# Attention then a squared-ReLU layer on one core: exp sums of batch 0's first query half as TensorE products by ones, and a new written order of the front

## The chip, the core and the metric

The kernel runs on one core of one Trainium2 chip. TensorE (PE in the profile) multiplies matrices out of the on-chip buffer into PSUM, VectorE (DVE) and ScalarE (ACT) do elementwise work, GpSimd (POOL) and SyncE (SP) issue most of the DMAs here. Each engine takes its own instructions from its own queue in the written order, and engines wait for one another by semaphores. The metric is device time in microseconds (us); lower is better. Times in the trace are counted from the start of the profiled span.

## The reference

```python
# q, k, v: (8 batches, 12 heads, 448 tokens, 64)
scores = scale * q @ k.T                 # per batch and head
e = exp(scores - max)
attn = e / (sum(e) + exp(-max) + 1e-9)   # softmax with a one added
x = (attn @ v) as (8 * 448, 768)
out = square(relu(x @ w_in)) @ w_out     # w_in 768 x 2048, w_out 2048 x 768
```

The kernel leaves out the maximum: it computes `exp(scores)`, and divides by the sum plus one.

## The kernel before, in words

A head is 64 wide, so most attention products are 64x64 tiles, four of which fit on TensorE's 128x128 array: two halves of rows, two halves of columns. The kernel groups four heads to a "quad" (`g`, three to a batch): a quad has two pairs `j` of heads and two heads `i` to a pair. The 448 keys are seven chunks `c` of 64.

Batch 0 is worked in two halves of 224 queries, so that work can begin early. A half of a quad (`half`, `g`) has four visits `k`, and visit number n = 12·half + 4·g + k (`HALVES`, L259). So n = 0 to 11 are the first half of quads 0, 1, 2, and n = 12 to 23 the second half. From n = 24 on come the quads of batch 1, with seven visits each. Visits with k = 3 hold one chunk instead of two; in the first half of quad 0 (`pieces`, L262) visits 0 and 1 take pair j = 0 and visits 2 and 3 take pair j = 1, so that each lies in one half of the columns when it is multiplied by the values.

The order of the first part is written out by hand as a string, `ORDER` (L858); a loop (L875) calls one function for each word. A word is a letter and numbers; each issues instructions on one engine, and the engine runs them in that order. The words that matter here:

| word | function | engine | what |
|---|---|---|---|
| `c`, `t`, `u` | `first_cast`, `first_transpose`, `first_copy` | ACT/DVE, PE, DVE/ACT | quad 0's queries and keys cast, transposed, copied |
| `Tb,g,n` | `transpose_one` (L204) | PE | 14 transposes of queries (n=0) or keys (n=1) of quad g, batch b |
| `Ub,g,n,c0,c1,act` | `transposed_copy` (L211) | DVE, or ACT with act=1 | chunks c0 to c1 of them, PSUM to the buffer |
| `sn` | `half_scores` (L272), `quad_scores` | PE | scores of a visit, 8 products at most, 4 for a visit with k = 3 |
| `en` | `half_exp` (L298), `quad_exp` | ACT | exp of a visit, 128x896 or 128x448 |
| `pn` | `post` (L313) | PE | exps times values of a visit; 28 products for a half of a quad |
| `bm,step` | `half_add` (L335) | DVE | four adds that bring the seven chunks of exps to one (m = 3·half + g) |
| `ym` | `half_sum` (L350) | PE | that one by ones: 4 products |
| `zm`, `nm` | `half_z` (L362), `half_reciprocal` (L371) | ACT | Ln(sum + one), exp of the negative |
| `xm` | `half_x` (L375) | DVE | values' products times the reciprocal |
| `ihalf,pair` | `half_in` (L529) | PE | 12 products of `x` with `w_in` for one half of batch 0's queries |
| `j`, `k`, `l`, `r`, `g` | `later_in` and its ReLU and square | PE, ACT or DVE, DVE | the first layer's products and what follows them |
| `dn` | a load | POOL | one or two DMAs |
| `S0` | `sums_of_quad` (L449) | PE | first sums of batch 1 |

Three PSUM pools bind the front. `s_psum` (L62) has two buffers: scores n can only be written when the exp of the visit that held the buffer has run. `x_psum` (L64) has one buffer, a pair of banks, for values and sums of a half of a quad: the next half of a quad waits for `x` of the one before. `m_psum` (L65) has two banks, for transposes and other products; the first half of quad 1 keeps its values and sums there.

From `S0` on nothing in the order of the words differs between the two kernels. The `d` words, the loads, stand in the same order in both.

Of the kernel before, what the change touches and what calls it, by code (L numbers as in the profile page):

```python
# [17 lines left out]
def kernel(  # L18
# [183 lines left out]
    tps = {}  # L202
# [651 lines left out]
    def other_ring():  # L854
# [240 lines left out]
```

## Time and profile before

| | |
|---|---|
| median of 3 runs | 372.84 us (372.32 to 373.31) |
| the profiled execution's own time | 372.36 us |
| its span in the profile | 370.3 us |
| PE busy | 361.7 us, 98% of the span |
| ACT busy | 282.4 us, 76% |
| DVE busy | 275.7 us, 74% |
| granted TensorE clock | 1.0 throughout |

The span is shorter than the time by 2.06 us, which lie around it. Busy PE time counts a matmul from its start to its modelled end, so overlapping products and gaps smaller than a pipeline's depth are not seen in it; the start times of the rows tell more. A row of the timeline gives the start, the time from the first start to the last end of a run of like instructions, engine, line, operation, shape and count, and in brackets the engine's idle time before it with what ended that.

### The profile page before, as it was taken

To read this page: it belongs to the slowest core of one execution; us is meant where nothing else is said; L and a number is where in the kernel's file an instruction comes from. 1 tells how busy PE (TensorE), PEld (TensorE's weight loads), DVE (VectorE), ACT (ScalarE), POOL (GpSimd) and SP (SyncE) were. 2 spreads that over 40 slices of the span, in tenths; PEclk is the share of its full clock that TensorE was granted. 3 is DMA by queue.
4 is the path that set the end of the run, shared out by engine and by line. 5 is a ranking of instruction groups with operands and counts; after the bars stand their busy time and mean duration, and the time that the engine had idled before them with its cause. 6 is when DMAs were issued, how large, how long until landed. Compare 5 with 4: busy or idle time off the path is not lost.

```text
span 370.3 us, 13666 instructions
## 1 busy us (share of the span) xinstructions
PE 361.7 (98%) x6024; PEld 248.8 (67%) x6024; DVE 275.7 (74%) x484; ACT 282.4 (76%) x413; POOL 62.3 (17%) x96
## 2 busy tenths in 40 slices
PE   8789999999999999999999999999999999999996
PEld 4566556669977755567799965557777765555664
DVE  3888898999987875867887874777878777885441
ACT  6899988987899645689999665679999748794221
POOL 8543350400400330400201060400200000000000
PEclk9999999999999999999999999999999999999999
DMA  8999999999777999905229669854212110001232
GB/s 138 203 205 205 204 198 206 226 225 189 154 146 133 190 181 191 134 2 114 62 58 156 154 118 180 162 64 99 61 53 66 47 62 5 2 0 44 86 85 88
DMA packets 75052, 45.31 MB, mean 122 GB/s; under 512 B 47473, under 2 KB 72945, under 8 KB 74993
## 3 DMA queue, kind: packets, MB, share of 16 engines
q0 software_dynamic: 24752, 22.62, 38.7%
q1 hardware_dynamic: 49952, 21.59, 27.0%
q8 instruction: 47, 0.77, 0.9%
q10 hardware_dynamic: 288, 0.23, 0.2%
q14 instruction: 13, 0.10, 0.1%
HBM read 45.69 MB, written 17.93 MB: 172 GB/s over the span
## 4 chain that ended last, share of the span: by engine, by line
PE 90%; ACT 4%; DVE 2%; DMA 2%; issue 1%; POOL 1%; POOLq 0%; DVEq 0%
PE mp L94 42%; PE mp L663 38%; PE sp L94 9%; ACT et L255 3%; DMA nn<-in_k_dram 2%; PE mp L208 1%; ACT rcp L373 1%; DVE qk L218 0%; ACT rcp L366 0%; DVE half L342 0%; DVE half L441 0%; DVE half L443 0%; DVE half L445 0%; DVE half L348 0%; DVE xt L485 0%
## 5 line engine op out<-in xcount | busy, mean ns | idle before, releaser
L255 ACT ACTIVATE et<-sp 128x896 f16<-128x896 f32 (+2 forms) x173 | 145.2, 899 | 7.6 <-PE sp L94 6.9
L94 PE MATMUL mp<-wout,gs 64*64 64x384 f16 (+1 forms) x2736 | 138.8, 322 | 0.2 <-issue 0.2
L94 PEld LDWEIGHTS <-gs 64*64 64x64 f16 (+1 forms) x2736 | 87.4, 107 | 21.7 <-issue 0.8
L663 PEld LDWEIGHTS <-win 128*128 128x128 f16 x480 | 46.4, 98 | 33.6 <-issue 1.2
L94 PE MATMUL sp<-qk 64*64 64x224 f16 (+1 forms) x1056 | 56.2, 273 | 2.3 <-issue 0.7
L663 PE MATMUL mp<-xt,win 128*128 128x448 f16 (+1 forms) x288 | 54.2, 329 | 0.0
L94 PEld LDWEIGHTS <-qk 64*64 64x64 f16 x1056 | 34.4, 114 | 14.5 <-issue 6.2
L189 POOL COPY flatq<-qk 64x384 f16<-64x384 f16 x20 | 15.3, 763 | 159.4 <-DMA qk<-stage_k 142.7
L94 PE MATMUL mp<-et,vn 64*64 64x448 f16 (+1 forms) x616 | 38.8, 345 | 0.0
L663 PE MATMUL mp<-et,win 128*128 128x448 f16 x144 | 32.8, 352 | 0.0
L576 DVE TENSOR_SCALAR ot<-mp 128x384 f32<-128x384 f32 x34 | 18.9, 556 | 18.0 <-PE mp L94 17.9
L663 PE MATMUL mp<-et,nn 128*128 128x448 f16 (+1 forms) x160 | 32.3, 350 | 0.0
L663 PEld LDWEIGHTS <-nn 128*128 128x128 f16 x216 | 21.0, 98 | 14.7
L666 ACT ACTIVATE qk<-mp 128x448 f32<-128x448 f32 (+1 forms) x33 | 16.8, 532 | 16.0 <-PE mp L663 15.9
L580 DVE SCALAR_TENSOR_TENSOR ot<-mp,ot 128x384 f32<-128x384 f32 x42 | 23.4, 556 | 6.7 <-ACT ot L574 4.0
L485 DVE TENSOR_TENSOR xt<-mp,rcp 128x448 f16<-128x448 f32 x42 | 24.2, 618 | 4.3 <-ACT rcp L464 2.2
L94 PEld LDWEIGHTS <-vn 64*64 64x64 f16 x756 | 22.7, 107 | 6.1 <-issue 0.5
L715 ACT ACTIVATE gs<-mp 128x448 f16<-128x448 f32 x28 | 14.2, 543 | 15.0 <-PE mp L663 13.3
L439 DVE TENSOR_TENSOR half<-et 128x1792 f16<-128x1792 f16 x21 | 23.0, 1097 | 1.2 <-ACT et L255 1.2
L660 DVE CUSTOM_DVE_ANT_0 gs<-mp,rcp 128x448 f16<-128x448 f32 x24 | 14.2, 619 | 13.0 <-ACT rcp L666 7.4
L441 DVE TENSOR_TENSOR half<-half,et 128x1792 f16<-128x1792 f16 x21 | 22.8, 1085 | 0.7 <-DVE half L439 0.5
L710 ACT ACTIVATE gs<-gs 128x448 f16<-128x448 f16 (+1 forms) x36 | 22.4, 657 | 1.1 <-DVE gs L660 1.1
(102 smaller groups left out, 450.2 us busy)
## 6 DMA issues: line engine op xcount, KB each, us to landing
out_dram<-ot SPq DMA_DIRECT2D x52, 96.0 KB, 3.5
out_dram<-ot SPq DMA_DIRECT2D x19, 192.0 KB, 2.0
win<-in_moe_w_in_dram POOLq DMA_DIRECT2D x8, 384.0 KB, 12.9
wout<-in_moe_w_out_dram POOLq DMA_DIRECT2D x4, 768.0 KB, 11.8
vn<-in_v_dram POOLq DMA_DIRECT2D x10, 288.0 KB, 5.6
stage_q<-in_q_dram POOLq DMA_DIRECT2D x4, 676.0 KB, 11.6
stage_k<-in_k_dram POOLq DMA_DIRECT2D x4, 676.0 KB, 14.4
nn<-in_q_dram POOLq DMA_DIRECT2D x8, 224.0 KB, 7.9
```

What stands on the lines that cost most here:

```text
L94: return nc.tensor.matmul(out_, lhsT, rhs, start=start, stop=stop)
L189: nc.gpsimd.tensor_copy(km[rows_].rearrange("p h (x o) -> p h x o", o=2)[:, :, :, odd], src[:, :, S // 2 - 32:S // 2])
L255: nc.scalar.activation(out=out_, in_=in_, func=AF.Exp, scale=scale)
L439: nc.vector.tensor_add(esq[m], a[:, 0:w], a[:, w:2 * w])
L441: nc.vector.tensor_add(esq[m], esq[m], z[:, 0:w])
L485: nc.vector.tensor_mul(xts[b][:, 2 * g + i, :], xqs[m][i][:, 0:S], zqs[m][:, i, :])
L576: nc.vector.tensor_scalar(out=ot, in0=op[:, 0:w], scalar1=OUT_SCALE, scalar2=None, op0=ALU.mult)
L580: nc.vector.scalar_tensor_tensor(out=ot, in0=lo[:, 0:w], scalar=OUT_SCALE, in1=ot, op0=ALU.mult, op1=ALU.add)
L660: nc.vector._custom_dve(TENSOR_ADD_SAT, out=out_, in0=ps, in1=t, s0=3.0e38, s1=0.0)
L663: nc.tensor.matmul(out_, lhsT=lhsT, rhs=rhs, start=begins and first, stop=last, skip_group_check=not begins)
L666: nc.scalar.activation(out=t[:, 0:w], in_=src[:, 0:w], func=AF.Copy, scale=scale_)
L710: nc.scalar.activation(out=out_, in_=out_, func=AF.Square)
```

## The change

The sums of the exps of the first query half (n = 0 to 11) are no longer made by adds on DVE (`b0`, `b1`, `b2`) and one set of four products (`y0`, `y1`, `y2`). `post` now also multiplies each piece of exps by ones, right behind its products by the values, into the sums' half of the same PSUM bank. For the second half of the queries nothing changes. `transposed_copy` may now copy the chunks in any order. The words before `S0` are ordered anew; two ReLUs swap engines (`k16` from ACT to DVE, `k17` from DVE to ACT).

```diff
     def transposed_copy(b, g, which, c0=0, c1=KC, act=0):
-        tp = tps.pop((b, g, which)) if c1 == KC else tps[b, g, which]
+        tp = tps[b, g, which]
+        copied[b, g, which] = copied.get((b, g, which), 0) + c1 - c0
+        if copied[b, g, which] == KC:
+            del tps[b, g, which]
...
                 mm(xz[i][64 * j:64 * j + 64, 0:FIRST], vns[0][r, j, g, c, :], e[r, j, c], start=key not in opened, stop=False)
                 opened.add(key)
-
-    SUMS_ON_PE = ()
-    ess = {}
+        if half == 0:
+            for c, j in parts:
+                done[g, j] = done.get((g, j), 0) + 1
+                for i in range(2):
+                    r = slice(64 * i, 64 * i + 64)
+                    mm(xz[i][64 * j:64 * j + 64, FIRST:2 * FIRST], ones[r], e[r, j, c], start=False, stop=done[g, j] == KC)
+
+    done, ess = {}, {}
...
     def half_sum(g, half):
-        xz, e = xzs[g, half], half_e(g, half)
-        t = ess.pop((g, half))[:, 0:4 * FIRST].rearrange("p (j c n) -> p j c n", j=2, c=2)
-        parts = [t[:, :, 0], t[:, :, 1], e[:, :, 6]] if half in SUMS_ON_PE else [t[:, :, 0]]
-        for n, part in enumerate(parts):
-            for i in range(2):
-                for j in range(2):
-                    r = slice(64 * i, 64 * i + 64)
-                    mm(xz[i][64 * j:64 * j + 64, FIRST:2 * FIRST], ones[r], part[r, j], start=False, stop=(n == len(parts) - 1))
+        xz = xzs[g, half]
+        t = ess.pop((g, half))[:, 0:4 * FIRST].rearrange("p (j c n) -> p j c n", j=2, c=2)[:, :, 0]
+        for i in range(2):
+            for j in range(2):
+                r = slice(64 * i, 64 * i + 64)
+                mm(xz[i][64 * j:64 * j + 64, FIRST:2 * FIRST], ones[r], t[r, j], start=False, stop=True)
...
     ORDER = """
-        d0 W8 d8 d1 c1,4,0 c0,0,1 t0,0,0 c1,0,1 t1,0,0 u0,0,0,0 t1,0,4 u1,0,0,0 c0,4,1 u1,0,4,1 t0,0,4 d2 s0 t0,1,0 u0,0,4,1 u0,1,0,0 t1,1,0
-        u1,1,0,0 d10 d9 s1 t0,1,4 e0 t1,1,4 e1 s2 e2 u0,1,4,0 s12 e12 u1,1,4,0 T0,1,0 T0,1,1 U0,1,0,0,4,0 U0,1,1,0,4,0 U0,1,1,4,7,0
-        U0,1,0,4,7,0 s3 s4 p2 p0 e3 b0,0 e4 s6 p1 d18 p3 s5 e6 e5 b0,1 b0,2 T0,2,0 b0,3 y0 T0,2,1 U0,2,0,0,4,0 z0 n0 U0,2,1,0,4,0 b1,0 s8
-        U0,2,0,4,7,0 U0,2,1,4,7,0 x0 d3 d17 d16 b1,1 s9 d15 T1,0,1 e8 e9 U1,0,1,0,7,0 T1,0,0 U1,0,0,0,7,0 b2,0 s11 e11 s10 s13 e10 e13 s14 p8
-        b2,1 p4 d5 b2,2 p9 s7 e14 p10 b2,3 p11 y2 p5 e7 z2 b1,2 p6 s15 b1,3 p7 e15 y1 b3,0 n2 x2 b3,1 z1 s17 e17 b3,2 p12 p13 b3,3 n1 s18 p14
-        s16 e18 p15 x1 y3 T1,1,0 U1,1,0,0,7,0 e16 b4,0 z3 b4,1 s19 e19 i0,6 n3 r0,6,0 s20 e20 s21 i0,7 s22 x3 b4,2 e21 p16 b4,3 e22 b5,0
-        r0,7,0 p17 p18 p19 d4 b5,1 g0,6 y4 z4 n4 s23 T1,1,1 e23 d13 s27 b5,2 x4 i0,4 s28 p20 p21 g0,7 b5,3 e27 p22 p23 y5 U1,1,1,0,7,0 e28 z5
-        r0,4,0 n5 x5 s26 s29 e26 j20,0,2 j23,0,2 j23,2,4 j20,2,4 j20,4,6 e29 j23,4,6 s25 k23,1 s24 g0,4 e25 e24 k20,0 P0 i1,7 j19,0,2 l23 a0,0
-        s32 e32 a0,1 s36 d6 j19,2,4 e36 j16,0,2 l20 j19,4,6 j17,0,2 s34 s33 k19,1 r1,7,0 j17,2,4 j16,2,4 a0,2 l19 e34 j17,4,6 e33 j16,4,6 g1,7
-        s30 d11 k16,1 s31 e30 k17,0 T2,0,0 T1,2,0 T2,0,1 T1,2,1 l16 s35 e31 U2,0,0,0,7,0 U1,2,0,0,7,0 s37 U2,0,1,0,7,1 e35 j18,0,2 j18,2,4 e37
-        j18,4,6 a0,3 i1,6 d19 S0 U1,2,1,0,7,0 v0,0 a1,0 v0,1 Z0 v0,2 l17 v0,3 v0,4 v0,5 k18,0 d7 d12 v0,6 s40 s43 M0 r1,6,0 j27,0,2 a1,1 e43
+        c1,4,0 c0,0,1 W8 d0 c1,0,1 c0,4,1 t0,0,0 t1,0,0 u0,0,0,0 d8 u1,0,0,0 t1,0,4 t0,0,4 u1,0,4,1 u0,0,4,1 d1 s0 d2 t0,1,0 t1,1,0 u0,1,0,0 s1
+        u1,1,0,0 e0 e1 t0,1,4 s2 t1,1,4 u0,1,4,0 d10 s12 T0,1,0 e2 u1,1,4,0 e12 U0,1,0,4,7,0 s13 T0,1,1 s14 e13 d9 U0,1,1,0,4,0 s3 e14
+        U0,1,1,4,7,0 U0,1,0,0,4,0 s4 d18 T0,2,0 e3 s5 U0,2,0,0,4,0 e4 e5 T0,2,1 s6 U0,2,1,0,4,0 s8 d3 e6 U0,2,1,4,7,0 e8 d17 p2 p3 d16 s10
+        U0,2,0,4,7,0 p0 p1 s17 b3,0 e10 T1,0,1 s19 T1,0,0 e17 s7 U1,0,1,0,7,0 z0 U1,0,0,0,7,0 e19 e7 p4 s11 n0 s9 p5 p6 p7 e11 e9 x0 d15 b3,1 z1
+        p8 s15 p9 s21 p10 e15 p11 d5 n1 s20 z2 e20 b3,2 x1 s22 n2 e21 T1,1,0 x2 T1,1,1 s16 p12 e22 e16 p13 d4 p14 p15 b3,3 s18 y3 U1,1,1,0,7,0
+        i0,7 e18 z3 s27 s24 U1,1,0,0,7,0 b4,0 n3 b4,1 i0,6 d13 b4,2 d6 e27 x3 e24 p16 s23 b4,3 e23 p17 p18 p19 r0,7,0 y4 b5,0 z4 b5,1 s26 n4 d11
+        i0,4 b5,2 e26 s32 e32 x4 p20 p21 p22 p23 b5,3 y5 s28 s33 z5 g0,7 r0,6,0 d19 n5 r0,4,0 e28 g0,6 e33 j20,0,2 j23,0,2 g0,4 j23,2,4 j20,2,4
+        x5 j23,4,6 j20,4,6 k20,0 k23,1 s30 s25 P0 i1,7 j17,0,2 e30 s29 e25 s31 l23 r1,7,0 j16,0,2 j19,0,2 a0,0 e29 j19,2,4 j17,2,4 j19,4,6
+        j17,4,6 j16,2,4 j16,4,6 s36 e31 a0,1 a0,2 s34 T1,2,1 k16,0 T1,2,0 k19,1 l19 g1,7 k17,1 T2,0,1 T2,0,0 e36 l16 U1,2,0,0,7,0 e34 l20
+        U2,0,0,0,7,0 s37 s35 j18,0,2 U2,0,1,0,7,1 a0,3 j18,2,4 e37 j18,4,6 i1,6 e35 S0 U1,2,1,0,7,0 v0,0 a1,0 v0,1 Z0 v0,2 l17 v0,3 v0,4 v0,5
```

More of the change, by code (lines that the diff above doesn't have):

```diff
@@ L200, in quad_columns @@
         return qk_of(b)[rows_, n, 2 * S * g:2 * S * (g + 1)].rearrange("p (i c x) -> p c i x", i=2, c=KC)
-    tps = {}
+    tps, copied = {}, {}
     def transpose_one(b, g, which):
@@ L867 @@
-        s32 e32 a0,1 s36 d6 j19,2,4 e36 j16,0,2 l20 j19,4,6 j17,0,2 s34 s33 k19,1 r1,7,0 j17,2,4 j16,2,4 a0,2 l19 e34 j17,4,6 e33 j16,4,6 g1,7
-        s30 d11 k16,1 s31 e30 k17,0 T2,0,0 T1,2,0 T2,0,1 T1,2,1 l16 s35 e31 U2,0,0,0,7,0 U1,2,0,0,7,0 s37 U2,0,1,0,7,1 e35 j18,0,2 j18,2,4 e37
-        j18,4,6 a0,3 i1,6 d19 S0 U1,2,1,0,7,0 v0,0 a1,0 v0,1 Z0 v0,2 l17 v0,3 v0,4 v0,5 k18,0 d7 d12 v0,6 s40 s43 M0 r1,6,0 j27,0,2 a1,1 e43
-        j22,0,2 j22,2,4 j27,2,4 X0 e40 j27,4,6 l18 j22,4,6 g1,6 a1,2 s39 k27,1 s38 e39 a1,3 d20 d21 d22 d14 d23 T2,2,0 e38 k22,0 T2,2,1 T2,1,1
@@ L871 @@
-        T2,1,0 s41 U2,2,1,0,7,1 U2,2,0,0,7,0 s42 j26,0,2 l27 e41 j21,0,2 j26,2,4 j26,4,6 l22 U2,1,0,0,7,0 j21,2,4 j21,4,6 i1,4 e42
-        U2,1,1,0,7,0 k26,1 k21,1 l26 l21 r1,4,0 g1,4
+        c1,4,0 c0,0,1 W8 d0 c1,0,1 c0,4,1 t0,0,0 t1,0,0 u0,0,0,0 d8 u1,0,0,0 t1,0,4 t0,0,4 u1,0,4,1 u0,0,4,1 d1 s0 d2 t0,1,0 t1,1,0 u0,1,0,0 s1
+        u1,1,0,0 e0 e1 t0,1,4 s2 t1,1,4 u0,1,4,0 d10 s12 T0,1,0 e2 u1,1,4,0 e12 U0,1,0,4,7,0 s13 T0,1,1 s14 e13 d9 U0,1,1,0,4,0 s3 e14
+        U0,1,1,4,7,0 U0,1,0,0,4,0 s4 d18 T0,2,0 e3 s5 U0,2,0,0,4,0 e4 e5 T0,2,1 s6 U0,2,1,0,4,0 s8 d3 e6 U0,2,1,4,7,0 e8 d17 p2 p3 d16 s10
@@ new lines @@
+        x5 j23,4,6 j20,4,6 k20,0 k23,1 s30 s25 P0 i1,7 j17,0,2 e30 s29 e25 s31 l23 r1,7,0 j16,0,2 j19,0,2 a0,0 e29 j19,2,4 j17,2,4 j19,4,6
+        j17,4,6 j16,2,4 j16,4,6 s36 e31 a0,1 a0,2 s34 T1,2,1 k16,0 T1,2,0 k19,1 l19 g1,7 k17,1 T2,0,1 T2,0,0 e36 l16 U1,2,0,0,7,0 e34 l20
+        U2,0,0,0,7,0 s37 s35 j18,0,2 U2,0,1,0,7,1 a0,3 j18,2,4 e37 j18,4,6 i1,6 e35 S0 U1,2,1,0,7,0 v0,0 a1,0 v0,1 Z0 v0,2 l17 v0,3 v0,4 v0,5
+        k18,0 d7 d12 v0,6 s40 s43 M0 r1,6,0 j27,0,2 a1,1 e43 j22,0,2 j22,2,4 j27,2,4 X0 e40 j27,4,6 l18 j22,4,6 g1,6 a1,2 s39 k27,1 s38 e39 a1,3
@@ L873 @@
+        d20 d21 d22 d14 d23 T2,2,0 e38 k22,0 T2,2,1 T2,1,1 T2,1,0 s41 U2,2,1,0,7,1 U2,2,0,0,7,0 s42 j26,0,2 l27 e41 j21,0,2 j26,2,4 j26,4,6 l22
+        U2,1,0,0,7,0 j21,2,4 j21,4,6 i1,4 e42 U2,1,1,0,7,0 k26,1 k21,1 l26 l21 r1,4,0 g1,4
     """
```

## The prediction

> **What bounds the kernel now.** I read the busy time by stretches first, to see which engine has no room in which stage, then the timeline of ScalarE and of TensorE through the front, then the waits in it.
>
> ```profile
> 20.00:30.00 10.00, 8.59 (x204) 6.74 (x203) 8.77 (x20) 9.96 (x18) 4.06 (x6) 1.00 1.24 204
> 30.00:40.00 10.00, 9.81 (x114) 5.81 (x110) 7.21 (x14) 9.35 (x14) 3.74 (x6) 1.00 1.26 205
> 40.00:60.00 20.00, 20.00 (x303) 12.26 (x306) 17.14 (x34) 17.76 (x24) 6.70 (x9) 1.00 1.29 201
> 60.00:345.00 285.00, 284.72 (x4952) 199.43 (x4945) 221.09 (x366) 224.80 (x326) 34.25 (x52) 1.00 0.59 110
> ```
>
> Columns: the stretch, its length, then busy time of PE, weight loads, DVE, ACT and POOL, the granted clock, DMA share and GB/s. From 20 to 40 us ACT has next to no idle time; from 40 to 345 us PE has 0.28 us of 305 idle, at clock 1.00. So there are two regimes: a front that ACT paces, in which PE waits now and then, and a body in which PE never waits. What is late or early on PE where the body begins is late or early at the end, one for one. The place to compare is `S0`, since behind it both kernels have one order:
>
> ```profile
> 47.32 0.38 PE L94 MATMUL sp<-half,ones 64*64 64x448 f16 x4
> ```
>
> In before it starts at 47.32. I ask when the changed kernel reaches it.
>
> **What the change adds on PE.** The half of a quad has 28 products by the values, so `post` adds 3 x 28 = 84 products by ones and the three `y` of 4 go: 72 more.
>
> ```profile
> 28.54 0.84 PE L94 MATMUL xp<-et,vn 64*64 64x224 f16 x28
> 29.21 0.27 PE L94 MATMUL xp<-half,ones 64*64 64x224 f16 x4
> ```
>
> 28 such products take 29.21 - 28.54 = 0.67 us, four at a time on the array, 0.024 each: 72 x 0.024 = 1.7 us. That is the price if nothing hides it; the lower end is nothing, if all fall into waits of PE.
>
> The upper end comes from quad 0. Its visits put all their products in one half of the columns, where only two run at a time.
>
> ```profile
> 11.15 0.58 PE L94 MATMUL xp<-et,vn 64*64 64x224 f16 x16
> 11.89 0.48 PE L94 MATMUL xp<-et,vn 64*64 64x224 f16 x12
> ```
>
> These are `p2 p0` and `p1 p3` of before: 8 products for the one column half, then 8 for the other. A product of 224 columns streams in 4 x 0.024 = 0.096. Two at a time, 16 would take 7 x 0.096 + 0.26 (the tail of one) = 0.93; the row has 0.58, so the later ones ran beside the earlier. In the new order `p2 p3` (14 by values and 14 by ones, one column half: 14 x 0.096 = 1.3 us) stand ahead of `s10`, and `p0 p1` (the same in the other half) behind it. If they too run beside each other, quad 0 costs no more than another; if not, up to 1.3 us more. I take the row's side.
>
> The Trainium skill speaks against that: TensorE: Matmul & The Clock Gate, Part 3, "The mechanism", says that matmuls keep strict program order in start and end, and only weight loads are pulled ahead. The 0.58 above does not agree for products in different tiles; by the page the sum would be up to 1.3 us worse, which is the slower rival below.
>
> **What it removes on DVE.**
>
> ```profile
> L344 DVE TENSOR_TENSOR half<-half,et 128x896 f16<-128x896 f16 x6 | 3.7, 620 | 0.2
> L342 DVE TENSOR_TENSOR half<-et 128x896 f16<-128x896 f16 x6 | 3.7, 619 | 0.0
> ...
> L348 DVE TENSOR_TENSOR half<-half,et 128x448 f16<-128x448 f16 x6 | 2.3, 391 | 0.3
> L346 DVE TENSOR_TENSOR half<-half 128x448 f16<-128x448 f16 x6 | 2.3, 388 | 0.1
> ```
> ```profile
> PE xp L94 <- DVE half L348: 0.5, 2, 0.3
> PE sp L94 <- DVE qk L218: 0.5, 1, 0.5
> ```
>
> The columns of the first are count, busy us, mean ns of one; of the second the total us, times and longest of a wait from 8 to 37 us. Half of each group goes: 3 x (0.620 + 0.619 + 0.391 + 0.388) = 6.05 us of DVE. But the last two lines show that PE lost only 0.5 to these adds and 0.5 to copies queued among them. DVE is not the pace; the gain is at most 1.0 us of PE waits, which fall where PE waits for ACT anyway. I count nothing for it by itself.
>
> **What moves.** ACT's order is worth a walk, with durations from these rows (start of one to start of the next):
>
> ```profile
> 20.61 0.64 ACT L366 ACTIVATE rcp<-xp,one_b 128x448 f32<-128x448 f32 x1
> 21.15 0.54 ACT L255 ACTIVATE et<-sp 128x448 f16<-128x448 f32 x1
> 21.57 0.58 ACT L373 ACTIVATE rcp<-rcp 128x448 f32<-128x448 f32 x1
> 22.04 0.79 ACT L369 ACTIVATE rcp<-mp,one_b 128x224 f32<-128x224 f32 x2
> 22.70 0.94 ACT L255 ACTIVATE et<-sp 128x896 f16<-128x896 f32 x1
> 23.49 0.60 ACT L373 ACTIVATE rcp<-rcp 128x448 f32<-128x448 f32 x1
> 23.96 1.75 ACT L255 ACTIVATE et<-sp 128x896 f16<-128x896 f32 x2
> 25.56 0.68 ACT L366 ACTIVATE rcp<-xp,one_b 128x448 f32<-128x448 f32 x1
> ```
>
> Exp of 896: 0.80. Of 448: 0.43. `z` 0.53, quad 1's `z` 0.66, `n` 0.47. An exp can follow its scores by 0.44, as 37.99 and 38.43 show here:
>
> ```profile
> 37.99 0.57 PE L94 MATMUL sp<-qk 64*64 64x448 f16 x8
> ```
> ```profile
> 38.43 1.73 ACT L255 ACTIVATE et<-sp 128x896 f16<-128x896 f32 x2 [0.49 <-PE sp L94]
> ```
>
> The start of the front, in before:
>
> ```profile
> 6.63 0.77 DVE L245 COPY qk<-mp 64x512 f16<-64x512 f16 x2 [1.29 <-PE mp L235]
> ...
> 8.33 1.73 ACT L255 ACTIVATE et<-sp 128x896 f16<-128x896 f32 x2 [0.29 <-PE sp L94]
> ...
> 9.83 0.58 PE L208 MATMUL mp<-ident,nn 128*64 128x128 f16 x14 [0.55 <-DMA nn<-in_k_dram]
> ...
> 10.86 3.22 ACT L255 ACTIVATE et<-sp 128x448 f16<-128x448 f32 x5 [0.81 <-PE sp L94]
> ```
>
> ACT idles 0.29 before `e2` (its scores stand behind a transpose) and 0.81 before `e3`, while PE waits at 9.83 for quad 1's keys. In the new order `s2` stands ahead of that transpose and can follow the copies that end at 6.63 + 0.77 = 7.40: `e2` at about 8.06, 0.27 earlier. `e13` and `e14`, which need quad 0 alone, fill the 0.81: `e12` 8.9, `e13` 9.7, then `s14` behind the transposes of 9.83, so `e14` 10.8 (0.2 idle), `e3` 11.6, `e4` 12.3, `e5` 13.1. Now `s6` stands behind the transposes of quad 2's keys (`T0,2,1`). These land two loads and a load of values after quad 1's:
>
> ```profile
> nn<-in_q_dram POOLq DMA_DIRECT2D x8, 224.0 KB, 7.9
> ```
>
> At 205 GB/s 224 KB take 1.12 us, so 9.8 + 3 x 1.12 = 13.15 (an estimate from these rows); `e6` at 14.2, idle 0.3. `e8` 15.0. Then `p2 p3` hold one column half to about 15.9, so `s10` ends late and `e10` comes at 16.3, idle 0.4; `p0 p1` beside it let `e17` go at 17.1. New waits queue here: behind `s10` stand all of PE, and behind `e10` all of ACT; that is the 0.4.
>
> From there ACT has no gap to `e16`: 5 exps of 896 (4.0), 4 of 448 (1.7), two `z` and quad 1's (1.7), three `n` (1.4): 8.9, so `e16` at 26.0. In before `e16` is the second exp of the row at 23.96, at 24.76; but the new order has by then done `e19`, `e20`, `e21`, `e22` and not yet `e18`: 0.43 + 2 x 0.80 = 2.0 more. Like for like 26.8 against 26.0: ACT is 0.8 ahead.
>
> PE: `s18` waits for `e22` to 26.1, `y3` follows at 26.6 and `i0,7` at 26.75.
>
> ```profile
> 25.30 1.32 PE L94 MATMUL mp<-xt,win 128*128 128x224 f16 x12
> ...
> 27.07 1.32 PE L94 MATMUL mp<-xt,win 128*128 128x224 f16 x12
> 28.32 0.39 PE L94 MATMUL sp<-qk 64*64 64x224 f16 x8
> ```
>
> A group of 12 takes 28.32 - 27.07 = 1.25, so `i0,7` and the change of width behind it are over at 28.0. Before is through it at 28.32, with `i0,6` (1.25) done as well, but without `s22` (0.2) and `T1,1,1`:
>
> ```profile
> 29.50 0.58 PE L208 MATMUL mp<-ident,nn 128*64 128x128 f16 x14
> 30.01 0.38 PE L94 MATMUL sp<-qk 64*64 64x448 f16 x4
> ```
>
> which took 0.51. Like for like 28.32 - 1.25 + 0.2 + 0.5 = 27.8: PE is 0.2 behind. Of the 1.7 us, 1.5 fell into its waits.
>
> From 28.0 on: the single buffer of `x_psum` holds `p20` until `x4`. ACT reaches `n4` at about 31.7, `x4` ends near 32.9, PE would be there at 32.5: 0.4 idle. After `z5` and `n5` (ACT at 35.2) `x5` ends near 35.9, and `j23,4,6` waits 0.2 for it. In return a wait of before goes:
>
> ```profile
> 32.56 0.81 PE L94 MATMUL sp<-qk 64*64 64x448 f16 x8
> 33.30 0.36 PE L94 MATMUL mp<-xt,win 128*128 128x448 f16 x1
> ```
>
> 33.30 - 32.56 = 0.74 for 8 scores that stream in 8 x 0.048 = 0.38, and 0.1 for the change of width: 0.26 of waiting. A change between 64- and 128-wide products costs that 0.1 (1.25 against 12 x 0.096), and the new order gathers the scores before `S0` into three groups instead of four: two changes fewer. 0.2 + 0.4 + 0.2 - 0.26 - 0.2 = 0.3: `S0` at 47.6.
>
> Weights do not bind: the issues at 29.36, 32.90 and 37.20, each waiting for a piece of `w_in`, show when those landed, and the products that read them start later in either order (31, 34 and 38.4).
>
> ```profile
> 29.36 0.70 POOL L118 DMA_DIRECT2D nn<-in_k_dram  x1 [2.36 <-DMA win<-in_moe_w_in_dram]
> ...
> 32.90 0.70 POOL L118 DMA_DIRECT2D nn<-in_q_dram  x1 [1.02 <-DMA win<-in_moe_w_in_dram]
> ...
> 37.20 0.69 POOL L106 DMA_DIRECT2D vn<-in_v_dram  x1 [1.61 <-DMA win<-in_moe_w_in_dram]
> ```
>
> The loads keep their order on POOL. `k16` and `k17` swap engines at one price. Both cost nothing.
>
> **Sum.** +1.7 added, -1.4 hidden: +0.3 us on the profiled execution, 372.36 (span 370.3, 2.06 around it), so 372.7. The median of the runs is 0.48 above that execution; the forecast against it is 373.1.
>
> **Rivals.** *Slower: the pairs of quad 0 run strictly one after the other.* Then `p0 p1` begin when `p2 p3` and `s10` are over, `s17` and with it `e17` come 0.7 late by the walk, up to 1.3 if ACT can't take any of it back; it decides as soon as `e17` starts later than 17.2. For it: with twice as many products the run in one column half is 28 long, where the rows show 8. Against: 0.58 and 0.48 above. Time: 373.1 + 1.2 = 374.3. *Faster: the waits that I placed aren't there.* If ACT's 0.9 (before `e14`, `e6`, `e10`) does not come, `x4` and `x5` are early as well and PE's 0.6 goes: 1.5 us, 371.6. For it: each of my waits is under 0.5 us and hangs on a landing or an order that before's trace doesn't show. Against: `s14` and `s6` do stand behind transposes whose data comes by DMA.
>
> **How the numbers follow.** A measurement here tells some 0.3% (1.1 us) from no change. Forecast, 373.1 with its own errors of half a microsecond a step: 0.5. Slower rival: 0.28. Faster rival: 0.22. The range reaches to both rivals and a little past them: 371.2 to 374.7. Faster by over 0.3% (under 371.7): 0.22; within: 0.5; slower (over 374.0): 0.28.
>
> **What would show it.** In the new profile: `S0`'s row (the first four products `sp<-half,ones` of 448) at 47.6; an exp at 9.7 where before idles; ACT idle of 0.2 to 0.4 before the exps near 10.8, 14.2 and 16.3, and hardly any from 17 to 26; PE idle before the first `xp<-et,vn` row near 33. The 28 products of `p2 p3` and those of `p0 p1` together in 1.5 to 2.2 us say that they ran beside each other; near 3 says they didn't. The prediction is wrong if PE is not dense from 38 us on, or if the granted clock falls in the sparse stretch from 9 to 17 us.

## The result and the profile after

The changed kernel takes 375.12 us, median of 10 runs (374.21 to 377.72); the kernel before took 373.04 in the runs beside it (10 runs, 372.32 to 373.40). The ratio is 1.0069, 95% interval 1.0049 to 1.0088: slower by about 2 us, where I had forecast 373.1 and a range up to 374.7. The profiled execution took 374.84 us, span 373.1, against 372.36 and 370.3. Before's is one of its quicker executions (0.68 under the median of 373.04; the changed kernel's is 0.28 under its own), so the profiled pair lies 2.5 us apart and the medians 2.1.

First `S0`, the point that the prediction named. The timeline of TensorE in the changed kernel (start, duration, operation, shape, count):

```profile
48.94 0.38 PE L94 MATMUL sp<-half,ones 64*64 64x448 f16 x4
```

It was 47.32 before and forecast at 47.6. So 1.62 of the span's 2.8 us were lost ahead of `S0`, 1.2 behind it, where the two kernels have one order and I had expected nothing. One profile is good to a few tenths here: in three more profiled executions of before's front (the runs with added DMAs below) `S0` starts at 46.84, 46.94 and 47.71. Next ScalarE's walk, the exps of the timeline:

```profile
7.84 7.96 ACT L258 ACTIVATE et<-sp 128x224 f16<-128x224 f32 x11
16.20 0.92 ACT L258 ACTIVATE et<-sp 128x896 f16<-128x896 f32 x1 [0.40 <-PE sp L94]
17.53 0.92 ACT L258 ACTIVATE et<-sp 128x896 f16<-128x896 f32 x1 [0.41 <-PE sp L94]
...
24.78 1.74 ACT L258 ACTIVATE et<-sp 128x896 f16<-128x896 f32 x2
27.08 1.78 ACT L258 ACTIVATE et<-sp 128x896 f16<-128x896 f32 x2 [0.56 <-PE sp L94]
```

Eleven exps end at 15.80 with no idle time worth a row: `e13` and `e14` do fill the hole before `e3`. `e10` comes at 16.20 with the 0.40 of idle time that I had put there. Then two rows differ: `e17` waits 0.41 more (17.53, not 17.1), and `e16` starts at 27.08, not 26.0, behind an idle time of 0.56 that I hadn't. On TensorE the same stretch reads:

```profile
22.74 0.39 PE L94 MATMUL sp<-qk 64*64 64x224 f16 x8
24.49 0.39 PE L94 MATMUL sp<-qk 64*64 64x224 f16 x8 [1.37 <-ACT et L258]
24.81 0.97 PE L208 MATMUL mp<-ident,nn 128*64 128x128 f16 x27
26.50 0.22 PE L208 MATMUL mp<-ident,nn 128*64 128x128 f16 x1 [0.72 <-issue]
26.64 0.39 PE L94 MATMUL sp<-qk 64*64 64x224 f16 x8
```

Of 28 transposes 27 run, and the last one starts 0.94 us late (0.72 behind the modelled end of the others). Its releaser is `issue`: no semaphore holds it. `s16` and with it `e16` stand behind it. The same sign stands once more in the body:

```profile
82.68 0.65 PE L94 MATMUL mp<-wout,gs 64*64 64x384 f16 x9
84.13 0.35 PE L94 MATMUL mp<-wout,gs 64*64 64x384 f16 x3 [0.80 <-issue]
```

Start to start 1.12 us are lost there. Along the body, the lag behind before's rows goes from 1.62 at `S0` to 2.7 at 84.13, back by 0.36 near 109, and to 2.8 at the end. Near 109 it is before that stalls, by 0.50 from start to start, and this kernel does not:

```profile
108.23 0.67 PE L94 MATMUL mp<-wout,gs 64*64 64x384 f16 x12
109.08 0.36 PE L94 MATMUL mp<-wout,gs 64*64 64x384 f16 x4 [0.18 <-issue]
```

**The number of the instruction.** Counted in order in the traces (a matmul is two instructions, weights and product, and the few semaphore instructions of TensorE's queue are one each), all these stalls stand ahead of instruction 193 + 256k: 961 and 3009 here, 705 and 3777 in before. The page's queue table (packets, MB, share) and its first part say why:

```profile
PE 364.4 (98%) x6096; PEld 252.6 (68%) x6096; DVE 271.4 (73%) x472; ACT 282.4 (76%) x413; POOL 61.5 (16%) x96
...
q8 instruction: 47, 0.77, 0.9%
```

47 packets of 16 KB in a queue of kind "instruction"; 2 x 6096 instructions of TensorE by 256 are 47.6. I read this as blocks of 256 instructions, 64 bytes each, that are fetched by DMA. I call the first instruction of a block an edge. Before's own timeline had held the sign, ahead of a wait that hid it:

```profile
21.17 0.38 PE L94 MATMUL sp<-qk 64*64 64x224 f16 x6
22.23 0.28 PE L94 MATMUL sp<-qk 64*64 64x224 f16 x2 [0.68 <-issue]
22.85 0.58 PE L94 MATMUL xp<-et,vn 64*64 64x224 f16 x16 [0.34 <-DVE xt L381]
```

Six of eight scores run, 0.93 are lost, and it cost nothing, since the products behind them waited for `x2` anyway. In all of these stalls the course is one: TensorE passes an edge, the transfer of a block starts about 3 to 4 us later, takes about 0.95, and 1.3 to 1.5 after its end the next edge passes (starts of TensorE's instructions and of queue 8's packets, us):

| kernel | edge | passed at | transfer starts | next edge at | stall there |
|---|---|---|---|---|---|
| before | 449 | 16.00 | 19.85 | 22.23 | 0.93 |
| after | 449 | 15.63 | 18.32 | 20.59 | none |
| after | 705 | 20.59 | 24.22 | 26.50 | 0.94 |
| after | 2753 | 77.67 | 81.72 | 84.13 | 1.12 |
| before | 9409 | 266.67 | 266.93 | 271.53 | none |

So in the front 256 instructions take 5 to 6 us at the least, 0.04 to 0.05 a product, while four 64-wide products of 224 columns side by side need 0.024 each. The theory: **the 144 added instructions press against the rate at which TensorE's code arrives, and shift every later edge onto another product.** Rivals: the order itself is slow; quad 0's pairs run one after the other (the prediction's slower rival); the clock falls in the sparse front.

### The profile page after: what moved, and what is told of

The parts are those of the page before. It is cut to its first block, busy times and chain, and to the rows that moved or that the text cites. A ratio compares the mean times of both kernels' runs of the same rounds, so it can differ in the third digit from the quotient of the medians.

```text
span 373.1 us, 13794 instructions
## 1 busy us (share of the span) xinstructions
PE 364.4 (98%) x6096; PEld 252.6 (68%) x6096; DVE 271.4 (73%) x472; ACT 282.4 (76%) x413; POOL 61.5 (16%) x96
## 4 chain that ended last, share of the span: by engine, by line
PE 90%; ACT 3%; DMA 2%; DVE 1%; POOL 1%; issue 1%; POOLq 0%; DVEq 0%; ACTq 0%
PE mp L94 42%; PE mp L669 37%; PE sp L94 9%; DMA nn<-in_k_dram 2%; ACT et L258 1%; PE mp L208 1%; PE xp L94 1%; ACT rcp L372 1%; ACT rcp L379 1%; POOL nn L118 1%; DVE xt L387 0%; DVE gs L510 0%; DVE half L449 0%; DVE half L451 0%; ACT ot L580 0%
## 5 line engine op out<-in xcount | busy, mean ns | idle before, releaser
L258 ACT ACTIVATE et<-sp 128x896 f16<-128x896 f32 (+1 forms) x173 | 145.1, 899 | 8.2 <-PE sp L94 7.5
L94 PEld LDWEIGHTS <-gs 64*64 64x64 f16 (+1 forms) x2736 | 89.1, 107 | 21.0 <-issue 1.2
L94 PE MATMUL sp<-qk 64*64 64x224 f16 (+1 forms) x1056 | 57.4, 273 | 2.0 <-ACT et L258 1.8
L189 POOL COPY flatq<-qk 64x384 f16<-64x384 f16 x20 | 14.3, 717 | 160.5 <-DMA qk<-stage_k 138.2
L94 PE MATMUL mp<-et,vn 64*64 64x448 f16 (+1 forms) x616 | 39.7, 345 | 0.4 <-DVE qk L221 0.4
L94 PEld LDWEIGHTS <-vn 64*64 64x64 f16 x756 | 24.1, 107 | 6.5 <-issue 1.3
L467 ACT ACTIVATE rcp<-sp,one_b 128x896 f32<-128x896 f32 x21 | 21.2, 1009 | 2.6 <-PE sp L94 2.5
```

The lines of the kernel that those rows point to most:

```text
L94: return nc.tensor.matmul(out_, lhsT, rhs, start=start, stop=stop)
L189: nc.gpsimd.tensor_copy(km[rows_].rearrange("p h (x o) -> p h x o", o=2)[:, :, :, odd], src[:, :, S // 2 - 32:S // 2])
L258: nc.scalar.activation(out=out_, in_=in_, func=AF.Exp, scale=scale)
L467: nc.scalar.activation(out=rcp, in_=zp[:, :, 0:S], func=AF.Ln, bias=one_b)
```

## The experiments

### The parts alone, and the edges alone

`sums_only` is before's order with the products by ones; `order_only` the new order with the adds. `after_w62` and `before_w77` leave the work and its order alone and put tiny products that nothing reads at the very start, in place of warming ones.

```diff
 sums_only:  ORDER of before, words b0,* b1,* b2,* y0 y1 y2 out; post and half_sum of after
 order_only: ORDER of after, with b0,* b1,* b2,* y0 y1 y2 put in; post and half_sum of before
 after_w62:  -W8   +D62 W3
 before_w77: -W8   +D77 W2
+    def spare(n, w=16):                      # the word D
+        for x in range(n):
+            y, z = slice(64 * (x % 2), 64 * (x % 2) + 64), slice(64 * (x // 2 % 2), 64 * (x // 2 % 2) + 64)
+            mm(aside()[z, x % 2, 0:w], idle[y, z], idle[y, 0:w], start=True, stop=True)
```

> Before's written order with the products by ones in post, the adds b0 to b2 and the y0 to y2 left out of it. Two theories. Fetch theory: PE takes its instructions in blocks of 256 (a matmul is two, weights and product), a block lands 5 to 6 us after the one before it was begun, and the 144 added instructions both press against that in the front and move every later block edge; then the body has the changed kernel's stall near 84 us (1.1 us) and not before's near 109 us (0.5 us), and S0 is about 1.0 late of 47.32: in all +1.8, a median near 374.8. Order theory: the new written order makes the loss; then this kernel is within 0.3 of before's 373.0.

Measured: 375.62, ratio 1.0065 [1.0039, 1.0090]. `S0` at 50.09, 2.8 late, not 1.0. Its stalls lie at 449 (0.92), 705 (0.24), 961 (0.95), 2753 (0.73), 3009 (1.26) and, against the expectation, at 3777 near 111 us (0.48). So the products cost this much without the new order. Whether they cost more in before's order is not shown: the medians, 375.62 and 375.12, lie in each other's intervals, and the profiled execution is the slowest of its eight (376.68).

> The new written order with the sums by adds on DVE (b0 to b2, y0 to y2 put back where their exps and values' products allow). Fetch theory: the instruction count is that of before, so the body has before's stall near 109 us (0.5) and none near 84 us; in the front the stall of 0.94 before the last transpose of batch 1's quad 1 goes or is hidden, quad 0's pairs cost 0.3 less: S0 near 47.5, median 373.2. Order theory: S0 stays near 48.9 and the median is 374.5 or more.

Measured: 377.54, ratio 1.0117 [1.0089, 1.0145], 3 us and more over the figure of either theory; the order theory's "374.5 or more" holds, though not its `S0` near 48.9. `S0` came at 50.89, and stalls lie at 77.66, 84.13 and 109.66 (0.55, 1.02, 0.62), at the edges 2497, 2753 and 3521. The body's instructions and edges are before's, and in before's profile none of these three stalls: the place of an edge alone does not decide, it also matters when it comes, here 3.6 us later. The waits of TensorE from 8 to 50 us, and then the stretches, with the granted clock behind POOL's column:

```profile
PE sp L94 <- ACT et L258: 1.9, 2, 1.3
PE xp L94 <- DVE half L350: 1.6, 1, 1.6
```
```profile
20.00:25.00 5.00, 2.56 (x80) 1.68 (x69) 4.07 (x10) 3.61 (x9) 2.52 (x4) 1.00 1.25 203
25.00:30.00 5.00, 4.23 (x86) 3.64 (x86) 2.71 (x5) 3.83 (x6) 1.61 (x3) 0.66 1.24 206
```

In the new order `e9` stands behind `e11`, so quad 2's chain of adds starts late and holds `y2` for 1.6; TensorE is busy 2.56 of 5 us, and in the next 5 the granted clock is 0.66; all six runs have a mean clock of 0.991 to 0.995. So without the adds the new order is spared something that I had priced at nothing. Another place for the adds was not tried, so this is the price of this one, with its lower clock in it.

> The converse: the kernel before with 77 tiny products in the place of 6 of the 8 warming products, 142 instructions more, which gives its body the changed kernel's block edges. Fetch theory: a stall of about 1.1 us appears near 83 us at an out_first product, the one near 109 us goes; S0 within 0.5 of 47.3; median 373.4 to 374.0, 0.4 to 1.0 over before. Rival: no effect, 373.0.

Measured: 374.15, ratio 1.0024 [1.0009, 1.0040]; `S0` at 47.87 (0.55 late). Part of the edit I had not meant: with fewer warming products the start is slower. ScalarE's first exps in before and here:

```profile
6.27 1.77 ACT L255 ACTIVATE et<-sp 128x896 f16<-128x896 f32 x3
```
```profile
6.86 0.92 ACT L255 ACTIVATE et<-sp 128x896 f16<-128x896 f32 x1 [0.41 <-PE sp L94]
```

The 0.59 between them is the whole lateness at `S0`; no edge stalls in the front. Behind it, TensorE's timeline:

```profile
80.80 1.46 PE L94 MATMUL mp<-wout,gs 64*64 64x384 f16 x29
82.82 0.35 PE L94 MATMUL mp<-wout,gs 64*64 64x384 f16 x3 [0.56 <-issue]
```

The stall appears on the predicted instruction, 3009, with 0.89, and the one near 109 is gone, though no instruction of the work was touched. So moved edges, with a start that is 0.55 late, put a stall of this size where the changed kernel has it. As a sum it is no loss that I can tell: from `S0` on the lag grows from 0.55 to 1.03, and in the three more executions of before, against the same rows, it grows by 0.34 to 0.65 (up to 250 us), with stalls of 0.44, 0.44 and 0.57 at 2753 and 0.59, 0.85 and 0.57 at 3777. The median is 1.3 over before's 372.85, just past the 374.0 expected.

> The changed kernel with 62 tiny products (64x64 by 16 columns, never read) in the place of 5 of the 8 warming products at the start, where PE has nothing else to do: the order behind them is untouched, but 114 instructions more come ahead of it, so that the body has before's block edges to within one instruction. Fetch theory: the stall near 84 us (1.1) goes, one near 109 us (0.4 to 0.5) comes, and the front's stall of 0.94 falls into the wait ahead of s22 (S0 0.5 to 0.9 earlier, 48.0 to 48.4): median 373.4 to 374.0. Rival, that the 72 added products and the order cost what they cost wherever the edges lie: 375.1, unchanged, with both stalls at the same rows.

Measured: 378.20, ratio 1.0144 [1.0106, 1.0181]. The expected sign was wrong, the mechanism not: I had taken the earlier edges for hidden ones, without adding up blocks. `S0` is at 51.23.

```profile
23.43 0.29 PE L94 MATMUL xp<-et,ones 64*64 64x224 f16 x2
25.51 0.38 PE L94 MATMUL xp<-et,ones 64*64 64x224 f16 x6 [1.79 <-issue]
```

The edges lie at 13.86, 19.59 and 25.51, 5.7 and 5.9 us apart, and the last stall is 2.04 long. `S0` is 2.3 later than in the changed kernel. 0.7 of that is the slower start (`e10` at 16.90, 16.20 there), the rest came from moving edges by 114 instructions that run while TensorE has nothing to do: they cost by where the blocks then begin, not by time of their own. The stall near 84 stayed too (1.08), one of 0.57 stands at 77.87, against the expectation, and the one near 109 didn't come. The instruction held near 84 is the one at before's edge 2753, which passes in before's first profile and is held by 0.44 to 0.57 in the three others; here it comes 4 us later. Which of the loads beside it does that was not tried.

### Quad 0's pairs

`after_pairs` and its repetition `after_pairs2` issue the products of visits 2 and 0, then 3 and 1, turn by turn.

```diff
-        U0,2,1,4,7,0 e8 d17 p2 p3 d16 s10 U0,2,0,4,7,0 p0 p1 s17
+        U0,2,1,4,7,0 e8 d17 p2,0 p3,1 d16 s10 U0,2,0,4,7,0 s17
+    def post(*visits):
+        for products in zip(*(post_products(at) for at in visits)):
+            for p in products:
+                mm(*p)
```

> The changed kernel with the products of quad 0's visits 2 and 0, then 3 and 1, issued turn by turn, so that both column halves of the array always have work; instruction count and all other words as they were. Theory of the pairs: they ran one after the other (2.5 us from the first product at 14.45 to the last at 16.98), side by side they take 1.4, e17 starts 0.5 earlier than 17.53 and S0 comes 0.4 to 0.5 earlier than 48.94. Fetch theory: e17 is 0.5 earlier too, but the block edge at instruction 705 then has to wait, since a block takes 5 us from the edge before it (15.6 to 20.6): S0 gains 0.2 at most, median 375 give or take 0.4.

Measured: 376.08, ratio 1.0092 [1.0063, 1.0122]; but in its profiled execution TensorE waited 1.4 us for the keys of quad 2, and the granted clock was 0.78 from 12 to 16 us and 0.79 to 20, which hides the pairs.

> The interleaved pairs of quad 0 once more, since in the profiled execution of the first one the keys of quad 2 landed 1.4 us late and the granted clock fell right behind, which hides what the pairs do. Pairs' theory: with the keys on time the last product of quad 0's visits ends by 16.5 (16.98 with the pairs one after the other), e17 at 17.0 and S0 at 48.5. Fetch theory: e17 at 17.0 too, S0 at 48.7 to 48.9, and the stall of 0.94 at edge 961 grows to 1.1 to 1.4.

Measured: 375.59, ratio 1.0073 [1.0052, 1.0095]. The timeline of TensorE:

```profile
14.23 0.55 PE L94 MATMUL xp<-et,vn 64*64 64x224 f16 x16
14.62 0.55 PE L94 MATMUL xp<-et,ones 64*64 64x224 f16 x16
15.00 0.46 PE L94 MATMUL xp<-et,vn 64*64 64x224 f16 x12
15.29 0.46 PE L94 MATMUL xp<-et,ones 64*64 64x224 f16 x12
15.57 0.55 PE L94 MATMUL sp<-qk 64*64 64x224 f16 x16
...
20.58 0.25 PE L94 MATMUL mp<-et,vn 64*64 64x224 f16 x1 [0.47 <-issue]
```
```profile
PE mp L208 <- issue: 1.0, 1, 1.0
PE mp L94 <- issue: 0.5, 1, 0.5
```

56 products take 15.57 - 14.23 = 1.34, where the changed kernel needed from 14.45 to 16.98 for them with `s10` and half of `s17` between. `e17` follows at 16.8. And `S0` comes at 49.23, not earlier than 48.94: the 0.7 us won come back as a stall of 0.72 at edge 705, and the one at 961 grows to 1.27. The pairs did run one after the other in the changed kernel, and it is not what it lost by.

### Fewer instructions: sums half by adds

Two adds bring six chunks of exps to two; three parts are multiplied by ones, 12 products instead of 28.

```diff
-        if half == 0:   (the products by ones in post)
+    SUMS_ON_PE = (0,)   (half_sum of before: t[:, :, 0], t[:, :, 1], e[:, :, 6])
 sums_half:  ORDER of before without b0,2 b0,3 b1,2 b1,3 b2,2 b2,3
 after_half: ORDER of after, with b0,0 b0,1 b1,0 b1,1 b2,0 b2,1 y0 y1 y2 put in (chunks 4 and 5 ahead of 2 and 3 for quad 2)
```

> Before's order with the same sums half by adds: 12 products by ones to a half of a quad, two adds of the four left out; 48 instructions more than before, 96 fewer than the run with all sums by products in before's order, whose S0 came 2.8 late with 2.1 us of stalls at three block edges. Fetch theory: the stalls shrink by more than the products, S0 0.5 to 1.2 late, median 373.2 to 374.5. Rival, cost in proportion to the products alone: 24 of 72, a third of 2.8, S0 0.9 late, and stalls at the same edges a third as long.

Measured: 373.55, ratio 1.0021 [1.0003, 1.0039]; `S0` at 48.34 (1.0 late, which fits the rival's 0.9 too), stalls 1.48 at 705 and 0.52 at 2753. The rival's stalls, a third as long at the same edges, are not there: 705 has six times the 0.24 of `sums_only`, 449 and 961 have none.

> The changed kernel's order, but with sums half by adds: two adds on DVE bring six chunks of exps to two, and three parts instead of seven are multiplied by ones, 12 products to a half of a quad where the changed kernel has 28 and before 4. 96 instructions fewer than the changed kernel. Fetch theory: in the dense front 96 instructions are worth up to 2 us at 5.5 us for 256; the stall of 0.94 near 26.5 goes, S0 near 47.6, and the body's edges lie 48 instructions behind before's, so a stall of 0.5 to 1.1 near 78 to 84 may stay: median 373.0 to 374.0. Rival, that the adds' chain on DVE is what matters: the adds for quad 2 hold y2 and with it s22, S0 at 49 or later.

Measured: 374.21, ratio 1.0041 [1.0024, 1.0059]; `S0` at 48.79, not 47.6, the stall at 961 down to 0.61 but not gone, none over 0.15 between 60 and 100 us, one of 0.34 at 3777. Both are nearer to before than their full versions, by 2.1 and 0.9 us. That instructions and products fall together here leaves the two apart only by the stalls' places; and `after_half` waits 1.2 for `x0` behind its adds on DVE, so its `S0` is no clean measure.

### The clock

`after_again` is the changed kernel once more, `after_warm` fills four idle places of TensorE.

```diff
 after_warm: s3 +W2 e14     s5 +W1     T0,2,1 +W1 s6     x1 +f4 s22
```

> The changed kernel unchanged, beside the other runs on the same chip, for more samples of its clock and of its stalls. Fetch theory: its profile has again a stall of 0.7 to 1.2 at block edge 3009, near 84 us, and none near 109; one of 0.5 to 1.0 at edge 961. Rival, that these stalls came by chance in the one profiled execution: they lie elsewhere or are gone. Median 375.1 give or take 0.5 either way.

Measured: 375.35, ratio 1.0079 [1.0053, 1.0106]. The stalls are there again: 0.62 at 705, 1.33 at 961, 0.70 at 3009, none near 109. And this profiled execution is one with a mean clock of 0.995, which six of the changed kernel's 19 runs have (376.46 to 377.78; the other 13 have a median of 374.84). Before has such runs too, but fewer: 7 of the 88 beside the experiments are under 0.999. The stretches and the timeline of TensorE show where:

```profile
24.00:28.00 4.00, 1.55 (x41) 0.95 (x35) 1.61 (x4) 3.48 (x5) 1.96 (x4) 0.91 1.26 200
28.00:32.00 4.00, 4.00 (x65) 3.28 (x68) 2.43 (x5) 2.52 (x4) 1.85 (x3) 0.66 1.24 208
```
```profile
25.45 0.39 PE L94 MATMUL sp<-qk 64*64 64x224 f16 x8 [1.34 <-ACT et L258]
25.77 0.97 PE L208 MATMUL mp<-ident,nn 128*64 128x128 f16 x27
27.85 0.26 PE L208 MATMUL mp<-ident,nn 128*64 128x128 f16 x1 [1.11 <-issue]
```

The wait of `s22` and the wait for code behind it leave TensorE 1.55 busy of 4 us, and the clock granted from 28 to 32 is 0.66. The Trainium skill, TensorE: Matmul & The Clock Gate, "HAM oscillation — how this bites in real kernels", asks for no idle gap over about 3.4 us; here shorter ones went ahead of the fall, 1.3 and 1.1 close together. In the changed kernel's first profile the same place has gaps of 1.37 and 0.72, TensorE is busy 2.79 of the 4 us, and the clock stays at 1.00.

> The changed kernel with warming products in four idle places of PE: two of 128x512 behind s3, one behind s5, one ahead of s6, and four of 128x448 ahead of s22; 16 instructions more. Theory that the gaps of the sparse front let the clock fall: of the changed kernel's 10 runs three had a mean granted clock of 0.995 and took 2.3 to 2.5 us more than the others; with the gaps filled no run has a clock under 0.999 and the median is that of its undisturbed runs, 374.6. Rival, the clock falls for another reason (a late DMA leaves PE without work for longer than the fill): two or three runs in ten stay at 0.995, median 375 or more.

Measured: 375.86, ratio 1.0072 [1.0048, 1.0097]. None of its six runs has a clock under 0.999, as the clock's theory says (by chance alone, at 6 in 19, one time in ten), but the fills cost as much as they save: `S0` 50.51, with a wait of 0.9 for code. So the cause of the lower clock is made likely by the traces and by these six runs, not shown.

### What makes a block slow

Late in before, from 253 to 301 us, blocks pass every 4.4 to 5.4 us without a stall. Three runs add DMAs there that nothing reads: five whole copies of each finished part of x; three copies in pieces of 128 bytes; DRAM to DRAM copies with a change of type, which the front's loads have as well.

```diff
 CYCLE of the last period:  X0 +t0 ... X1 +t1 ... X2 +t2 ... X3 +t3 ... X4 +t4
 before_dma:   t: 5 x dma(out=dump[x, n], in_=xts[b][:, 2 * g:2 * g + 2, :])
 before_dma2:  t: 3 x the same, out in rows of 64 elements
 before_dma3:  t0 to t3: 3 x dma(out=dump (float16), in_=q, 330 rows of 1024 float32)
```

> The kernel before with 25 DMAs added that nothing reads: behind each of five X words of the last period (about 255 to 300 us) the finished part of x, 229 KB, is written five times to DRAM. No instruction is added on TensorE, ScalarE or VectorE. In before that stretch takes a block of 256 instructions in 4.5 to 5.0 us without a stall, while the DMA engines are a fifth busy; in the front, with them full, a block takes 5.2 to 6.4. Fetch theory: the block waits behind other transfers, so with the added traffic the blocks take 5 to 6 us there and PE stalls at several edges by 0.3 to 1.0 each: 1 to 5 us in all. Rival, a block's time doesn't depend on the traffic: no change, 372.9.

> As the run before with extra DMAs, but each copy of a finished part of x goes to DRAM in pieces of 64 elements (128 bytes), three copies for each of five X words, 53760 bytes of descriptors' worth of small pieces for each X: the DMA engines should be at a share near 1.2, as they are in the front, and not 0.65, as they were with whole rows. Theory that a code block waits behind queued packets: its fetches come no closer than 5.5 to 6 us then, and PE stalls by 0.3 to 1.3 at several edges between 265 and 300 us, 1 to 5 us in all. Rival, full DMA engines don't matter either: no stall there; what makes the front's blocks slow is then open.

Measured: 372.65 and 372.77, ratios 0.9995 [0.9979, 1.0010] and 1.0000 [0.9982, 1.0017], no stall in that stretch. Before_dma, last two columns the share of the DMA engines and GB/s:

```profile
265.00:275.00 10.00, 10.00 (x276) 7.86 (x272) 8.64 (x15) 9.76 (x12) 6.85 (x12) 1.00 0.65 227
275.00:285.00 10.00, 10.00 (x276) 7.76 (x270) 8.05 (x12) 9.98 (x13) 2.66 (x5) 1.00 0.63 211
```

So GB/s are not it: 227 here without a stall, 205 in the front with stalls. But the engines are busy 0.65 (0.78 at most in `before_dma2`, whose pieces of 128 bytes went out as 1440 packets of 2.4 KB on average), in the front 1.24. Against the theory as stated, which had 1 to 5 us, and not yet at its condition.

> The kernel before with twelve DRAM to DRAM copies that nothing reads (676 KB each, float32 to float16 as the loads of the front are), three behind each of four X words of the last period, about 258 to 300 us. They should hold the DMA engines at a share of 1.2 for some 40 us, which the two runs with extra DMAs before it did not (0.65 and 0.75). Theory that a code block waits behind queued packets: its fetch starts 2 to 4 us behind the block's edge in that stretch (0.0 to 0.4 in before, up to 1.8 at a share of 0.75), blocks come no closer than 5.5 us, PE stalls at several edges by 0.3 to 1.3 with no semaphore in it: 1 to 6 us in all, beside waits that name a DMA or a store. Rival, full DMA engines do not matter: blocks at 4.4 to 5.0 us as in before and no stall without a semaphore.

Measured: 380.73, ratio 1.0216 [1.0188, 1.0245], 8.0 us where 1 to 6 were expected. The stretches, then all waits of TensorE from 255 to 320 us:

```profile
265.00:275.00 10.00, 9.68 (x262) 7.86 (x255) 8.21 (x13) 9.25 (x12) 3.90 (x7) 1.00 1.03 206
275.00:285.00 10.00, 7.51 (x200) 6.08 (x195) 6.68 (x11) 7.23 (x9) 2.21 (x4) 1.00 1.08 234
285.00:295.00 10.00, 9.10 (x244) 7.67 (x236) 6.37 (x10) 8.22 (x10) 2.21 (x4) 1.00 1.07 230
295.00:305.00 10.00, 8.11 (x200) 5.90 (x196) 6.05 (x10) 4.78 (x6) 0.00 (x0) 1.00 1.07 228
```
```profile
PE mp L94 <- issue: 3.8, 4, 1.3
PE sp L94 <- issue: 2.4, 3, 1.2
```

At a share of 1.03 to 1.08 every edge from 9665 to 11201 stalls, seven in a row: 0.58, 1.65, 1.51, 1.22, 1.25, 1.25, 0.91, together 8.4 us, and no wait in the stretch names a semaphore. The transfers start 3.2 to 4.0 us behind the edges (-0.2 to 0.4 in before from 262 us on), the blocks pass every 5.9 to 6.2 us. Nothing on TensorE changed: DMA engines that are full of these copies make the block slow.

Full engines alone are not the condition, though; before's own body has a stretch that tells. The share there, then what filled the engines in it, and from 20 to 30 us:

```profile
119.00:124.00 5.00, 5.00 (x132) 3.57 (x124) 3.64 (x7) 3.70 (x5) 0.00 (x0) 1.00 1.35 192
```
```profile
q1 hardware_dynamic: 3656, 0.92, 131.6%
```
```profile
q0 software_dynamic: 2134, 2.02, 123.5%
```

At a share of 1.35, over the front's 1.24, edge 4289 is passed at 118.52, a transfer starts at 119.42, 0.9 behind it, and edge 4545 comes at 123.53 without a stall. The packets are of queue 1 there, of 0.25 KB; in the front they are of queue 0, of 0.95 KB, and of the 1.08 in `before_dma3` from 275 to 285 us queue 0 has 0.90. So blocks come late beside loads of queue 0 that fill the engines. Which property of those loads does it was not tried.

`before_w55` moves the edges by 100 instructions:

```diff
 before_w55: -W8   +D55 W3
```

> The kernel before with 55 tiny products in the place of 5 warming ones at the start: 100 instructions more, so that the block edges of the body fall on other products than with 0 more (stall of 0.5 near 109, 0.1 to 0.4 near 79) and with 142 more (0.9 near 83). Fetch theory: with the edge near instruction 2909 of before the fourth block of the dense stretch has till 83 us, where PE slows down by itself, so no stall over 0.4 near 80 to 84, and the one near 109 moves or goes: 372.2 to 373.0, up to 0.5 faster than before. Rival, any shift costs about what 142 instructions cost: 373.5 to 374.5.

Measured: 373.71, ratio 1.0019 [1.0002, 1.0035]. `S0` is 0.68 late by the slower start (first exps at 7.12), none of the front's edges stalls, and behind it the lag grows by 0.5, as with 142 and as in before's own executions. The time is what the rival gave (373.5 to 374.5), not the 372.2 to 373.0 of the fetch theory. The stalls are 0.43, 0.36 and 0.29 at 2753, 3009 and 3777, instead of one of 0.89: at nearly the same lateness the place of the edges moves the stalls, but no shift that was tried gained time, and no kernel here beats the one before.

## Why the prediction was wrong, point by point

**The price of 72 products failed**, in the term "-1.4 hidden" of the sum. The text gave the price as 1.7 us "if nothing hides it; the lower end is nothing, if all fall into waits of PE". Products that fall into a wait are not free: each is two instructions of a block that takes 5 to 6 us to come while loads of queue 0 fill the DMA engines. `after_w62` shows it with instructions that cost no time of their own, `sums_only` with the products themselves. In the profiled pair this is about half of the 1.3 us by which `S0` missed its forecast: of the 0.94 at edge 961, 0.56 stand on the walk as ACT's idle time before `e16` (`s18` would have waited for `e22` in any case). 0.4 is the lateness of `e17`, 0.2 lies behind `i0,7`.

**"A body in which PE never waits" failed.** Late or early at `S0` was to carry to the end one for one. The body has waits that busy time doesn't show (0.28 us idle in 305, and 0.50 lost at one instruction), and they lie at the edges: +1.12 at 84 and -0.36 at 109. The place of the edges is one part of it, as `before_w77` shows; when they come is another. With the changed kernel's edges `sums_only` and `after_pairs2` do stall near 109 to 111 (0.48, 0.44), with before's edges `order_only` stalls at 84 (1.02). Whether before, only 1.6 late, would stall so too was not tried. Nor is all of the body's 1.2 the change: before's own executions differ by 0.34 to 0.65 there, the one profiled first being the quickest; the changed kernel's repetition lost 1.2 again. The 0.4 us left of the body's 1.2 are small steps (0.26 near 130, 0.17 near 241) whose cause stays open.

**The pairs: the slower rival's mechanism was right, its price not.** `e17` came at 17.53, past the 17.2 where the rival decides. I had taken the side of the rows 0.58 and 0.48, which show that products pass one another over a distance of about eight; here 28 stood in the way. The 2.5 us for the 56 lie between the two signs that the prediction gave (2.2 and 3), but they are two stretches one behind the other, from 14.45 to 15.7 and from 15.64 to 16.98, each the 1.3 that the prediction worked out for one column half alone. Taking the 0.4 away brought nothing (`after_pairs2`).

**What held.** The walk of ScalarE to `e10`, within 0.2: `e13` in the hole, 0.40 idle before `e10`. In part this is luck: the idle times of 0.2 and 0.3 before `e14` and `e6` did not come, and `e10` was only 0.1 earlier for it. From `e17` to the end of `e22` the walk's 8.9 us took 9.0. The stretch from the end of `i0,7` to `S0`: forecast 47.6 - 28.0 = 19.6, measured 48.94 - 29.17 = 19.8. The wait for `x4` in it is there, with 0.2 instead of 0.4:

```profile
PE xp L94 <- DVE xt L387: 0.2, 1, 0.2
```

**The removed adds** were counted at nothing by themselves. For before's order nothing here speaks against that; the new order, with the adds where `order_only` has them, is slower with them.

**The clock** was named as a danger for 9 to 17 us. In the changed kernel's one profiled execution that has it, it falls from 28 to 32, behind a gap that the wait for code helps to make; such runs, a third of all, take 2.6 us more (medians 377.4 and 374.8). In `after_pairs` it fell between 12 and 20 us, partly in the stretch that was named, with the keys 1.4 late. It is no part of the profiled pair, which has 1.00 throughout, and the other two thirds of the runs are 2 us slower than before without it.

## What to carry to other kernels

Where TensorE works in many small products while loads like the front's fill the DMA engines, count instructions as well as time: here 256 instructions, 128 products with their weights, need 5 to 6 us. Idle times with the releaser `issue`, on instructions that lie a multiple of 256 apart, are such waits, and one that another wait hides in before is a warning. A change that adds instructions moves every edge behind it, so a microsecond gained or lost far from the edit can come from there; shift the edges with instructions that do nothing to tell the two apart, see that the filling doesn't change the start, and take several profiles of the kernel before: one gave 0.15 where three others gave 0.44 to 0.57.

## What was not expected of the hardware

- TensorE's code comes in blocks of 256 instructions, and the fetch competes with the kernel's own loads: late in the kernel 4.4 to 5.4 us to a block pass without a stall at a DMA share of 0.14 to 0.78, 5.9 to 6.2 with stalls at 1.03 to 1.08. The Trainium skill, Runtime: NRT & Kernel Launch, "Instruction fetch mechanics", describes the blocks of 256, and says that crossing a boundary is mostly hidden. The trace agrees with the first (47 packets, stalls 256 apart). With the second it agrees for most edges (in before's profile 2 of 47 stall by more than 0.2 us), but not for the seven in a row of `before_dma3`, nor for the 2.04 us at one edge of `after_w62`.
- Neither bytes nor the engines' share alone tell: 227 GB/s at a share of 0.65 delayed nothing, 206 GB/s at 1.03 did, and a share of 1.35 with packets of queue 1 made no stall.
- Products of 64x64 tiles in different column halves overtook one another over about eight products, not over 28: turn by turn 56 of them took 1.34 us, one half after the other 2.5.
